# Feature attention and a gated MLP in one kernel: constants built on ScalarE or pinned later on VectorE, one load per step issued long ahead, crossbar transposes queued apart from their loads

## The chip, the cores and the metric

One core of one Trainium2 chip. The metric is the time of one execution on the device in microseconds (us); lower is better. Engines: PE is TensorE, DVE is VectorE, ACT is ScalarE, POOL is GpSimd, SP is SyncE. One digit of a slice in a profile is the share of busy time in tenths. The executions of the kernel before scatter widely: over the runs of this study, 296 to 307 us. So differences below 1% are told by spans of traces and by steps inside them, and a verdict on time only by ratios with an interval. A run is called slow when it lies over 1.5% above the fastest of the same kernel; ratios use the other, fast runs alone.

## The reference

```python
def phi(x):                                    # q, k: [8, 8, 576, 64]; w_phi: [64, 128]
    proj = np.einsum('bhsd,df->bhsf', x, w_phi)
    proj = proj - np.max(np.abs(proj), axis=-1, keepdims=True)
    return np.concatenate([np.exp(proj), np.exp(-proj)], axis=-1)
q_p, k_p = phi(q), phi(k)
kv = np.einsum('bhsf,bhsd->bhfd', k_p, v)
z = np.sum(k_p, axis=2)
num = np.einsum('bhsf,bhfd->bhsd', q_p, kv)
den = np.einsum('bhsf,bhf->bhs', q_p, z)[..., None] + 1e-06
x = (num / den).transpose(0, 2, 1, 3).reshape(8, 576, 512)
h = np.maximum(x @ w_in, 0.0)                  # w_in: [512, 1024]
u, v = h[..., :512], h[..., 512:]
v_n = (v - v.mean(-1)) / sqrt(var(v) + 1e-06)  # over the last axis
v_s = np.einsum('ts,bsd->btd', w_spatial, v_n) + b_spatial[None, :, None]
out = (u * v_s) @ w_out
```

## The kernel before

Of the 576 tokens of a batch, 512 form four *pair units* (two heads each); the last 64 tokens of two batches together form one *tail unit*. So there are 36 units, u0 to u35. One step of the program per unit: in step i, unit i's keys and queries are projected, later stages follow at fixed lags, and between them matmuls of the gated MLP (gMLP) of finished batches are dealt out as filler. The order within a step is `ORDER`, the dose of filler `RATE`. Tail units are u1, u9, u18 and u27; batch 4 begins at u19, batch 5 at u23, batch 6 at u28, batch 7 at u32.

Names in the profiles: k_bf, q_bf and v_f are the loaded keys, queries and values of a batch (k_tl, q_tl, v_tl of a tail unit); kT_b, qT_b (kT_t, qT_t of a tail) are their crossbar transposes, that is transposes made by a DMA. Up to batch 1 PE transposes them, and the result is copied to kT and qT. mk and mq are the maxima of keys and queries, kf and qf (qf_t) the exponentials, mhl the split of mq in two parts. em are the exponentials of mk, and vs (vst of a tail) is v scaled by them, x the normalised result of the attention and xT its transpose, w_spT the transposed w_spatial with the bias rows, ob a buffer for output rows. The feature lag is the number of steps between a unit's keys and its qf.

```python
    def load_heads(b, h0, n):                  # POOL loads and casts, SP transposes
        d = st[b]
        for x, t in (("k", k), ("q", q)):
            src = d[x][:, h0:h0 + n]
            pin(nc.gpsimd.dma_start)(out=src, in_=main_ap(t, b, h0, n))
            if b >= XB:
                pin(nc.sync.dma_start_transpose)(out=d[x + "T"][:, 2 * h0:2 * (h0 + n), :],
                                            in_=src.rearrange("p h x -> p (h x)"))
    # ... (cut)
    def a_split(u):
        m = mhl[u["i"] % NM]
        eng = nc.vector if u["i"] < EARLY else nc.gpsimd
        eng.tensor_copy(out=m[:, 0:H], in_=u["mq"])
        eng.tensor_tensor(out=m[:, H:2 * H], in0=u["mq"], in1=m[:, 0:H], op=ALU.subtract)
    # ... (cut)
    def o_mm(lhs, r):
        # ... (cut)
        ob = s2.tile([P, DM], FP32, tag="ob", name="ob", bufs=4)
        nc.scalar.copy(out=ob[r], in_=po[r])   # stored by SP; four buffers
        return ob
    # ... (cut)
    for i in range(NU + 4):
        u = unit(i)
        step(i)
        if i == 0:
            load(1)
            load_weights()
        if u and u["pair"] and u["pj"] == NP - 1 and u["b"] + 2 < B:
            load(u["b"] + 2)
        if u and u["pair"] and u["pj"] == TS and u["b"] % 2 == TB and u["g"] + 1 < G:
            load_tail(u["g"] + 1)
```

Of the kernel before, what the change touches and what calls it, by code (L numbers as in the profile page):

```python
# [16 lines left out]
def kernel(  # L17
# [40 lines left out]


    def pin(start):  # L60
        return lambda **kw: tc.keep_in_program_order(start(**kw))

    def main_ap(t, b, h0=0, n=H):
        return bass.AP(tensor=t.tensor, offset=t.offset + (b * H + h0) * S * D,
# [6 lines left out]
    st = {}  # L71
    gs = {}

    TS, TB = 1, 1
    XB = 2

    def load_tail(g):
        d = dict(
            q=ld.tile([P, H, D], BF16, tag="q_tl", name="q_tl", bufs=1),
            k=ld.tile([P, H, D], BF16, tag="k_tl", name="k_tl", bufs=1),  # L80
            v=ld.tile([P, H, D], FP32, tag="v_tl", name="v_tl", bufs=1),
        )
        gs[g] = d
        for x, t in (("k", k), ("q", q)):
            for i in range(2):
                pin(nc.gpsimd.dma_start)(out=d[x][i * TL:(i + 1) * TL], in_=tail_ap(t, 2 * g + i))
            if 2 * g >= XB:
                d[x + "T"] = ld.tile([P, NP, P], BF16, tag=x + "T_t", name=x + "T_t", bufs=1)
                pin(nc.sync.dma_start_transpose)(out=d[x + "T"], in_=d[x].rearrange("p h d -> p (h d)"))
        for i in range(2):  # L90
            pin(nc.sync.dma_start)(out=d["v"][i * TL:(i + 1) * TL], in_=tail_ap(v, 2 * g + i))

    def alloc(b):
        st[b] = dict(
            q=ld.tile([P, H, NB * D], BF16, tag="q_bf", name="q_bf", bufs=2),
            k=ld.tile([P, H, NB * D], BF16, tag="k_bf", name="k_bf", bufs=2),
            v=ld.tile([P, H * NB, D], FP32, tag="v_f", name="v_f"),
        )
        if b >= XB:
            for x in ("kT", "qT"):  # L100
                st[b][x] = ld.tile([P, 2 * H, P], BF16, tag=x + "_b", name=x + "_b", bufs=2)

    def load_heads(b, h0, n):
        d = st[b]
        for x, t in (("k", k), ("q", q)):
            src = d[x][:, h0:h0 + n]
            pin(nc.gpsimd.dma_start)(out=src, in_=main_ap(t, b, h0, n))
            if b >= XB:
                pin(nc.sync.dma_start_transpose)(out=d[x + "T"][:, 2 * h0:2 * (h0 + n), :],
                                            in_=src.rearrange("p h x -> p (h x)"))  # L110

    def load_v(b, eng):
        pin(eng.dma_start)(out=st[b]["v"].rearrange("p (h c) d -> p h (c d)", h=H), in_=main_ap(v, b))

    def load(b):
        alloc(b)
        load_heads(b, 0, H)
        load_v(b, nc.gpsimd if b < 2 else nc.sync)


    ident = cpool.tile([P, P], BF16)
    make_identity(nc, ident)
    alloc(0)
    for x, t in (("k", k), ("q", q)):
        first = s2.tile([P, 2, NB * D], FP32, tag="ob", name="first", bufs=4)
        nc.sync.dma_start(out=first, in_=main_ap(t, 0, 0, 2))
        nc.vector.tensor_copy(out=st[0][x][:, 0:2], in_=first)
    wphi2 = cpool.tile([P, 2 * F], BF16)
    nc.vector.memset(wphi2, 0.0)
    wphi_f = cpool.tile([P, F], FP32)  # L130
    for i in range(2):
        r = slice(i * D, (i + 1) * D)
        nc.sync.dma_start(out=wphi_f[r, :], in_=w_phi)
        nc.vector.tensor_copy(out=wphi2[r, i * F:(i + 1) * F], in_=wphi_f[r, :])
    load_tail(0)
    load_heads(0, 2, 2)
    load_v(0, nc.gpsimd)
    load_heads(0, 4, 4)

    w_in_bf = cpool.tile([P, KC, DFF], BF16)  # L140
    w_out_bf = cpool.tile([P, KC, DM], BF16)
# [5 lines left out]
    nc.sync.dma_start(out=bsp_row[TL:TL + 1, :], in_=moe_b_spatial)  # L147
    nc.sync.dma_start(out=bsp_row[0:1, :], in_=moe_b_spatial)

    def load_weights():  # L150
        pin(nc.gpsimd.dma_start)(out=w_in_bf, in_=moe_w_in.rearrange("(kc p) f -> p kc f", p=P))
        rows = moe_w_spatial[0:T0, :].rearrange("(p c) s -> p c s", c=NB)
        pin(nc.gpsimd.dma_start)(out=wsp, in_=rows[:, :, 0:T0])
        pin(nc.gpsimd.dma_start)(out=wspr, in_=rows[:, :, T0:S])
        pin(nc.gpsimd.dma_start)(out=wspt, in_=moe_w_spatial[T0:S, :])
        pin(nc.gpsimd.dma_start)(out=w_out_bf, in_=moe_w_out.rearrange("(kc p) f -> p kc f", p=P))


    sel1 = cpool.tile([P, H], BF16)
    sel = cpool.tile([P, H, F], BF16)  # L160
    nc.vector.tensor_tensor(out=sel1, in0=ident[:, 0:H], in1=ident[:, H:2 * H], op=ALU.add)
    nc.vector.tensor_scalar(out=sel, in0=sel1.unsqueeze(2).to_broadcast([P, H, F]), scalar1=-1.0,
                            scalar2=None, op0=ALU.mult)
    neghalf = cpool.tile([P, NB + 1], FP32)
    nc.vector.memset(neghalf, -0.5)


    NM = 3
    EARLY = 4
    XX = 9  # L170
    mhl, mT = [], []
    for i in range(NM):
        t = cpool.tile([P, P], BF16, name=f"mhl{i}")
        nc.vector.memset(t, 0.0)
        mhl.append(t)
        t = cpool.tile([P, P], BF16, name=f"mT{i}")
        nc.vector.memset(t, 0.0)
        mT.append(t)
    vst, vnt = [], []
    for i in range(2):  # L180
        t = cpool.tile([P, 2, 2, H, DA], BF16, name=f"vst{i}")
        nc.vector.memset(t, 0.0)
        vst.append(t)
        t = cpool.tile([P, 2, HALF], BF16, name=f"vnt{i}")
        nc.any.memset(t, 0.0)
        nc.any.memset(t[TL:TL + 1, 0, :], 1.0)
        nc.any.memset(t[0:1, 1, :], 1.0)
        vnt.append(t)
    nc.any.memset(w_spT[:, NB:NB + 2, :], 0.0)

    def transpose_spatial(i):

        pt = psum.tile([P, S], BF16, tag="bank", name="pt")
        if i < NB:
            sc = POS[i]
            for tp, c in enumerate(POS):
                nc.tensor.transpose(out=pt[:, tp * P:(tp + 1) * P], in_=wsp[:, c, bass.ds(sc, P, step=NB)],
                                    identity=ident)
            nc.tensor.transpose(out=pt[:, T0:S], in_=wspt[:, bass.ds(sc, P, step=NB)],
                                identity=ident[:TL, :TL])  # L200
            nc.vector.tensor_copy(out=w_spT[:, i, :], in_=pt)
            return
        for bl in range(2):
            lo = bl * TL
            for tp, c in enumerate(POS):
                nc.tensor.transpose(out=pt[lo:lo + TL, tp * P:(tp + 1) * P], in_=wspr[:, c, :], identity=ident)
            nc.tensor.transpose(out=pt[lo:lo + TL, T0:S], in_=wspt[:, T0:S], identity=ident[:TL, :TL])
            nc.vector.tensor_copy(out=w_spT[lo:lo + TL, NB + bl, :], in_=pt[lo:lo + TL, :])
        for bl, row in ((0, TL), (1, 0)):
            for pos, c in enumerate(POS):  # L210
                nc.vector.tensor_copy(out=w_spT[row:row + 1, NB + bl, pos * P:(pos + 1) * P],
                                      in_=bsp_row[row:row + 1, bass.ds(c, P, step=NB)])
            nc.vector.tensor_copy(out=w_spT[row:row + 1, NB + bl, T0:S], in_=bsp_row[row:row + 1, T0:S])


    def a_transpose(u):
        src = st[u["b"]] if u["pair"] else gs[u["g"]]
        if "kT" in src:
            for x in ("kT", "qT"):
                u[x] = src[x][:, 4 * u["pj"]:4 * u["pj"] + 4, :] if u["pair"] else src[x]  # L220
            return
        for x, copy in (("k", nc.scalar.copy), ("q", nc.vector.tensor_copy)):
            pt = psum.tile([P, 4, P], BF16, tag="bank", name="pt")
            for j in range(4):
                if u["pair"]:
                    blk = src[x][:, 2 * u["pj"] + j // 2, (j % 2) * P:(j % 2 + 1) * P]
                else:
                    blk = src[x][:, 2 * j:2 * j + 2, :]
                nc.tensor.transpose(out=pt[:, j, :], in_=blk, identity=ident)
            u[x + "T"] = a1.tile([P, 4, P], BF16, tag=x + "T", name=x + "T", bufs=2 if x == "k" else 4)  # L230
            copy(out=u[x + "T"], in_=pt)
# [296 lines left out]
    def unit(i):  # L528
        return units[i] if 0 <= i < NU else None
# [3 lines left out]
    def b_tasks(b):  # L533
# [15 lines left out]
        if tail:  # L549
# [5 lines left out]
            for x in bls:  # L555
                ts += [(mm, lambda j=j, x=x: b_o(2 * g + x, j)) for j in range(NB)]
        return ts

    ORDER = (("keys", 0.375), ("queries", 0), ("sums", 0), ("next", 0.125),
             ("attention", 0.5), ("features", 0), ("maxima", 0), ("out", 0))  # L560
    RATE = 3.23
    CAP = 1.76
    LAGS = dict(next=-1, maxima=1, features=2, sums=2, attention=3, out=4)
    FIRST = dict(next=-1, maxima=1, features=2, sums=2, attention=3, out=3)
    credit = [0.0]
# [1 line left out]
    def fill(share):  # L567
        credit[0] = min(credit[0] + RATE * share, CAP)
        while queue and credit[0] >= queue[0][0] / 2:
            cost, task = queue.pop(0)  # L570
            task()
            credit[0] -= cost

    def lag(u, what):
        return (FIRST if u["pair"] and u["b"] == 0 or u["i"] == 1 else LAGS).get(what, 0)

    def step(i):

# [32 lines left out]
    def finish_batch(u, f):  # L611
# [3 lines left out]
        elif bl == 1:  # L615
            f(g, [0, 1])

    for i in range(NU + 4):
        u = unit(i)
        step(i)  # L620
        if i == 0:
            load(1)
            load_weights()
        if u and u["pair"] and u["pj"] == NP - 1 and u["b"] + 2 < B:
            load(u["b"] + 2)
        if u and u["pair"] and u["pj"] == TS and u["b"] % 2 == TB and u["g"] + 1 < G:
            load_tail(u["g"] + 1)
    while queue:
        queue.pop(0)[1]()

# [29 lines left out]
```

## Time and profile before

| | before |
|---|---|
| median of the first 3 runs | 299.48 us (298.49 to 300.39) |
| span of the profiled run | 300.1 us |
| PE busy | 262.3 us |
| first gMLP product | 53.55 us |

The first gMLP product is the first matmul with w_in: from there PE has filler. The lines that bear the argument are in the prediction below. Here are two stretches that turn out to matter, from busy time by stretch (stretch and length; busy us and instructions of PE, weight loads, DVE, ACT, POOL; granted TensorE clock; DMA share; GB/s):

```profile
118.00:140.00 22.00, 18.33 (x207) 12.36 (x207) 12.80 (x34) 16.86 (x38) 12.58 (x23) 1.00 1.27 214
190.00:216.00 26.00, 24.17 (x278) 16.27 (x280) 18.49 (x45) 23.33 (x56) 14.30 (x27) 1.00 0.91 199
```

PE loses 3.7 and 1.8 us there, at full clock, though the DMA share is already 1.27 and 0.91.

### The profile page before, as it was taken

How to read it: one execution, taken by the hardware profiler on the slowest of the kernel's cores; microseconds unless marked ns; L12 is line 12 of the kernel's file. 1: busy time of each engine (PE TensorE's matmuls, PEld its weight loads, DVE VectorE, ACT ScalarE, POOL GpSimd, SP SyncE). 2: the span in 40 equal slices, each digit the busy share in tenths (PEclk: the TensorE clock that was granted, in tenths of full speed). 3: DMA queues.
4: the chain of work that ended last, by engine and by line, in shares of the span. 5: the costliest groups of instructions: out<-in, count | busy, mean ns of one | idle time of the engine just before them, and what ended most of it. 6: DMA issues, size and time to landing. Idle time of an engine off the chain costs nothing.

```text
span 300.1 us, 7883 instructions
## 1 busy us (share of the span) xinstructions
PE 262.3 (87%) x3007; PEld 180.4 (60%) x3046; DVE 211.9 (71%) x512; ACT 224.1 (75%) x512; POOL 184.1 (61%) x324
## 2 busy tenths in 40 slices
PE   2356888999999999779999995979999999999983
PEld 1235777576766766556667673656767667545441
DVE  5999889797968877549697883656788864445610
ACT  4336899878699997769999675879999837566033
POOL 9398388589635998447879962814988430048300
PEclk9999999999999999999999997999999999999998
DMA  9999999909952899999612999999303202600026
GB/s 142 245 153 268 166 111 159 262 1 123 215 190 75 109 166 233 152 280 162 136 21 28 185 211 224 142 305 235 81 1 37 20 2 69 226 26 0 0 84 233
DMA packets 82906, 41.10 MB, mean 137 GB/s; under 512 B 53490, under 2 KB 77234, under 8 KB 82868
## 3 DMA queue, kind: packets, MB, share of 16 engines
q1 hardware_dynamic: 55524, 27.08, 41.9%
q0 software_dynamic: 27344, 13.51, 33.1%
q8 instruction: 24, 0.39, 0.6%
q14 instruction: 14, 0.11, 0.1%
HBM read 32.85 MB, written 9.44 MB: 141 GB/s over the span
## 4 chain that ended last, share of the span: by engine, by line
PE 56%; DVE 16%; ACT 14%; DMA 8%; issue 3%; SPq 1%; ACTq 0%; DVEq 0%
PE ps L476 9%; PE pv L402 7%; PE pu L455 6%; PE po L499 6%; PE ps L236 6%; DMA out_dram<-ob 5%; ACT kf L251 5%; PE pn L353 3%; DVE mk L248 3%; DVE mq L257 3%; PE pv L333 3%; ACT qf L320 3%; PE pq L303 3%; PE pq L307 3%; PE ps L477 2%
## 5 line engine op out<-in xcount | busy, mean ns | idle before, releaser
L251 ACT ACTIVATE kf<-ps 128x512 bf16<-128x512 f32 x144 | 76.8, 667 | 19.4 <-DVE mk L248 19.1
L320 ACT ACTIVATE qf<-pq 128x512 bf16<-128x512 f32 x128 | 68.0, 667 | 13.6 <-PE pq L307 13.6
L268 POOL TENSOR_TENSOR vs<-v_f,em 128x512 bf16<-128x512 f32 x64 | 65.6, 1047 | 15.7 <-ACT em L263 15.5
L248 DVE TENSOR_REDUCE mk<-ps 128x4 f32<-128x512 f32 x72 | 46.1, 678 | 9.5 <-PE ps L236 9.2
L257 DVE TENSOR_REDUCE mq<-ps 128x4 f32<-128x512 f32 x72 | 46.3, 679 | 3.1 <-PE ps L236 2.7
L501 ACT COPY ob<-po 128x512 f32<-128x512 f32 (+1 forms) x37 | 21.6, 597 | 25.7 <-PE po L499 17.2
L405 DVE BATCH_NORM_STATS2 stats<-vr 128x6 f32<-128x512 bf16 (+1 forms) x37 | 25.2, 685 | 17.6 <-ACT vr L404 17.5
L402 PE MATMUL pv<-w_in_bf,xT 128*128 128x512 bf16 x119 | 31.2, 379 | 2.2 <-DMA xT<-x 1.7
L476 PE MATMUL ps<-w_spT,vn 128*128 128x512 bf16 x117 | 32.3, 379 | 0.6
L455 PE MATMUL pu<-xT,w_in_bf 128*128 128x512 bf16 x120 | 30.8, 379 | 0.7 <-DVE mq L257 0.3
L307 PE MATMUL pq<-mT,sel 128*128 128x128 bf16 x256 | 30.7, 222 | 0.0
L499 PE MATMUL po<-w_out_bf,uT 128*128 128x512 bf16 x121 | 29.7, 379 | 0.4 <-issue 0.2
L479 DVE TENSOR_TENSOR uT<-ps,uT 128x512 bf16<-128x512 f32 x32 | 22.1, 691 | 11.0 <-PE ps L477 9.7
L307 PEld LDWEIGHTS <-sel 128*128 128x128 bf16 x256 | 25.4, 99 | 6.5 <-issue 2.2
L344 DVE TENSOR_TENSOR x<-pn,rc 128x256 bf16<-128x256 f32 x64 | 25.8, 419 | 1.0
L287 POOL CAST mhl<-mq 128x8 bf16<-128x8 f32 x32 | 6.2, 192 | 33.1 <-DVE mq L257 29.3
L404 ACT ACTIVATE vr<-pv 128x512 bf16<-128x512 f32 (+1 forms) x37 | 23.2, 680 | 4.2 <-PE pv L402 3.3
L333 PE MATMUL pv<-vs,kf 128*128 128x66 bf16 x512 | 25.0, 195 | 0.0
L419 POOL TENSOR_SCALAR vn<-vr,rs 128x512 bf16<-128x512 bf16 x32 | 24.3, 772 | 0.8
L333 PEld LDWEIGHTS <-kf 128*128 128x128 bf16 x512 | 23.9, 99 | 1.0
L353 PE MATMUL pn<-kv,qf 128*128 128x66 bf16 x512 | 22.2, 193 | 2.0 <-ACT kf L251 0.9
L353 PEld LDWEIGHTS <-qf 128*128 128x128 bf16 x512 | 19.4, 97 | 6.0 <-issue 2.5
(127 smaller groups left out, 547.5 us busy)
## 6 DMA issues: line engine op xcount, KB each, us to landing
out_dram<-ob SPq DMA_DIRECT2D x32, 256.0 KB, 2.7
v_f<-in_v_dram SPq DMA_DIRECT2D x6, 1024.0 KB, 6.8
k_bf<-in_k_dram POOLq DMA_DIRECT2D x7, 512.0 KB, 6.7
q_bf<-in_q_dram POOLq DMA_DIRECT2D x7, 512.0 KB, 8.3
v_f<-in_v_dram POOLq DMA_DIRECT2D x2, 1024.0 KB, 8.5
v_tl<-in_v_dram SPq DMA_DIRECT2D x8, 128.0 KB, 4.2
w_in_bf<-in_moe_w_in_dram POOLq DMA_DIRECT2D x1, 1024.0 KB, 12.5
out_dram<-ob SPq DMA_DIRECT2D x8, 128.0 KB, 2.9
```

The source lines that it names most:

```text
L248: nc.vector.tensor_reduce(out=u["mk"][:, hs], in_=pk, axis=AX.X, op=ALU.max, apply_absolute_value=True)
L251: nc.scalar.activation(out=u["kf"][:, s, hs, :], in_=pk, func=AF.Exp, bias=0.0, scale=sc)
L257: nc.vector.tensor_reduce(out=u["mq"][:, 4 * half:4 * half + 4], in_=pq, axis=AX.X, op=ALU.max, apply_absolute_value=True)
L268: nc.gpsimd.tensor_tensor(out=vs[:, s, :, 0:D], in0=st[u["b"]]["v"][:, pj * H:(pj + 1) * H, :], in1=em[:, s, :].unsqueeze(2).to_broadcast( ...
L307: nc.tensor.matmul(out=pq[:, 2 * par + x, :], lhsT=sel[:, j, :], rhs=m, start=False, stop=(x == 1))
L320: nc.scalar.activation(out=qf[:, s], in_=pq, func=AF.Exp, bias=0.0, scale=sc)
L333: nc.tensor.matmul(out=pv[:, hh, s, :], lhsT=u["kf"][:, s, 4 * hh + c, :], rhs=u["vs"][:, s, 4 * hh + c, :], start=(c == 0), stop=False)
L353: nc.tensor.matmul(out=pn[:, pos, :], lhsT=u["qf"][hh][:, s, pos, :], rhs=d["kv"][:, 2 * u["pj"] + hh, s, :], start=(s == 0), stop=(s == 1))
L402: nc.tensor.matmul(out=pv[r], lhsT=lhs(kc), rhs=w_in_bf[:, kc, HALF:DFF], start=(kc == 0), stop=(kc == KC - 1))
L455: nc.tensor.matmul(out=pu, lhsT=w_in_bf[:, kc, dc * P:(dc + 1) * P], rhs=d["xT"][:, kc, :], start=(kc == 0), stop=(kc == KC - 1))
L476: nc.tensor.matmul(out=ps, lhsT=d["vn"][:, sp, cs], rhs=w_spT[:, sp, 0:T0], start=(sp == 0), stop=False)
L499: nc.tensor.matmul(out=po[r], lhsT=lhs(dc), rhs=w_out_bf[:, dc, :], start=(dc == 0), stop=(dc == KC - 1))
```

## The change

Its intent: (1) *constants*: get zero fills and casts out of VectorE's way at the start; (2) *loads and transposes*: spread the loads over the steps, long ahead, and queue the crossbar transposes so late that SP never sleeps behind its own loads; (3) *order*: new `ORDER`, `RATE`, `CAP`, and a feature lag of 3 for the first tail unit. The core of the diff (cuts marked; moved but equal lines left out):

```diff
-    def load_heads(b, h0, n):  ...            # load and crossbar transpose together
+    def cross(b):                             # crossbar transposes alone
+        d = st[b]
+        for x in ("k", "q"):
+            d[x + "T"] = ld.tile([P, 2 * H, P], BF16, tag=x + "T_b", name=x + "T_b", bufs=2)
+            pin(nc.sync.dma_start_transpose)(out=d[x + "T"], in_=d[x].rearrange("p h x -> p (h x)"))
 ...
-        nc.vector.memset(t, 0.0)              # vst
+        pin(nc.scalar.copy)(out=t.rearrange("p b s h d -> p (b s h d)"), in_=zero.to_broadcast([P, 4 * H * DA]))
 ...
-    EARLY = 4
+    EARLY = 6
+    EK = 7
+    AT, AB, XP, XQ = 6, 6, 3, 3
+    def constants(i):                         # on VectorE, after steps 1, 2 and 3
+        if i < 2:
+            for bl, row in ((0, TL), (1, 0)):
+                pin(nc.vector.tensor_copy)(out=vnt[i][:, bl, :], in_=ident[:, row:row + 1].to_broadcast([P, HALF]))
+        elif i == 2:
+            pin(nc.vector.memset)(w_spT[:, NB:NB + 2, :], 0.0)
 ...
-            for pos, c in enumerate(POS):     # bias casts: ten small ones become four
-                nc.vector.tensor_copy(out=w_spT[row:row + 1, NB + bl, pos * P:(pos + 1) * P], ...)
+            pin(nc.vector.tensor_copy)(
+                out=w_spT[r, NB + bl, 0:T0].rearrange("o (a b p) -> o a b p", a=2, b=2), ...)
 ...
-        for x, copy in (("k", nc.scalar.copy), ("q", nc.vector.tensor_copy)):
+        for x, copy in (("k", nc.vector.tensor_copy if u["i"] < EK else nc.scalar.copy), ("q", nc.vector.tensor_copy)):
 ...
-    ORDER = (("keys", 0.375), ("queries", 0), ("sums", 0), ("next", 0.125),
-             ("attention", 0.5), ("features", 0), ("maxima", 0), ("out", 0))
-    RATE = 3.23
-    CAP = 1.76
+    ORDER = (("keys", 0.375), ("queries", 0.25), ("sums", 0), ("attention", 0.25),
+             ("next", 0.125), ("features", 0), ("maxima", 0), ("out", 0))
+    RATE = 3.12
+    CAP = 2.11
 ...
+    for u in units:
+        if not u["pair"] and u["g"] > 0:
+            for n, (x, y) in enumerate((("k", 0), ("k", 1), ("q", 0), ("q", 1))):
+                at(u["i"] - AT + n, load_tail, x, u["g"], y)
+            ...
+            if 2 * u["g"] >= XB:
+                at(u["i"] - XQ, cross_tail, u["g"])
+        if u["pair"] and u["pj"] == 0 and u["b"] > 1:
+            at(u["i"] - AB, load, "k", u["b"])
+            at(u["i"] - AB + 1, load, "q", u["b"])
+            at(u["i"] - AB + 1, load_v, u["b"], nc.sync)
+            if u["b"] >= XB:
+                at(u["i"] - XP, cross, u["b"])
```

## The prediction

> **What bounds the kernel now.** I read the page's slices first, then busy time by stretch, then the chain of waits, then the waits of the stretches where TensorE (PE) is idle.
>
> ```profile
> PE   2356888999999999779999995979999999999983
> DVE  5999889797968877549697883656788864445610
> DMA  9999999909952899999612999999303202600026
> ```
>
> One digit is 7.5 us. PE is weak in the first six digits (45 us) and dips at 120 to 130, near 180 and near 195 us; elsewhere it is at 9. VectorE (DVE) is full where PE starts, and the DMA engines are busy there and in every dip. Busy time by stretch gives the sizes:
>
> ```profile
> 0.00:58.00 58.00, 37.87 (x460) 29.92 (x462) 49.80 (x121) 39.52 (x91) 41.75 (x69) 1.00 1.14 188
> 58.00:120.00 62.00, 61.18 (x756) 43.42 (x766) 50.62 (x124) 53.36 (x128) 46.76 (x84) 1.00 0.78 141
> 120.00:146.00 26.00, 21.74 (x283) 15.82 (x284) 17.47 (x46) 21.76 (x50) 16.38 (x29) 1.00 1.23 207
> 176.00:205.00 29.00, 23.58 (x300) 16.26 (x302) 16.23 (x40) 20.27 (x50) 14.06 (x24) 0.94 1.20 219
> ```
>
> PE idle is the length less the second number: 20.1 us before 58, 0.8 in the good stretch 58 to 120, 4.3 and 5.4 in the two bad ones. All of PE's idle time is 300.1 - 262.3 = 37.8 us; 5.9 more lies after 258 us, where only the last batch pair's products and stores remain. So the kernel is PE-bound, with a slow start and two stretches of stalls. What fills the start stands in the chain of waits, in order of time (start, us, what):
>
> ```profile
> 1.73 3.28 DMA wphi_f<-in_w_phi_dram
> ...
> 6.17 0.94 DVE vst L182
> 7.26 0.48 DVE vnt L186
> ...
> 9.24 0.69 DVE sel L162
> 9.93 0.33 DVE qT L231
> ...
> 15.14 0.96 DVE w_spT L213
> 16.12 1.05 DVE w_spT L211
> ...
> 53.55 1.37 PE pv L402 x5
> ```
>
> Up to 25 us the chain is DVE doing constants (vst, vnt, sel) and bias casts (w_spT) between the reduces that the pipeline needs. The copy of qT, ready to go at about 5.5 us, runs at 9.9. The last line is the first gMLP product; from there PE is rarely idle. The stalls later stand in the waits of PE, SyncE (SP) and ScalarE (ACT); the SP line is of the whole run, the others of 58 to 257 us (total, times, longest):
>
> ```profile
> PE ps L236 <- DMA kT_t<-k_tl: 5.1, 2, 3.4
> PE pv L402 <- DMA xT<-x: 1.7, 1, 1.7
> SPq L61 <- DMA k_bf<-in_k_dram: 75.8, 6, 39.5
> ACT ob L501 <- DMA out_dram<-ob: 5.4, 3, 2.8
> ```
>
> SP issues in order. A crossbar transpose (kT_b, kT_t) stands right behind its own load, so SP sleeps until the load has landed, and the xT transposes, v loads and output stores behind it sleep too.
>
> **What the Trainium skill says.** (1) "SBUF — State Buffer", Who interferes with whom: VectorE copies and casts in a 2-port mode and GpSimd (POOL) hold one port pair exclusively. The trace agrees: the 128x8 mhl cast takes 0.17 us at 13.45 and 1.27 us at 19.83, while POOL issues weight loads; the qT copy out of PSUM, at 19.50 in the same stretch, takes its usual 0.40. (2) "DMA: Bandwidth & Descriptors", Two DMAs through the same engine are not ordered: a DMA that reads what another wrote must have its issuing engine wait for the first one's semaphore. That is the 75.8 us above. (3) "ScalarE: Activation LUTs", Rules for kernel authors: about 0.3 us + 0.83 ns per element for one activation. The trace has 0.59 to 0.60 us for a 128x512 copy, less than the 0.72 of that rule. (4) "Perfetto Trace Analysis", Identifying the Most-Contended Engine: matmul busy time is no measure of distance from the peak. The trace agrees: 128x512 matmuls are recorded as 379 ns each, yet 16 of them take 3.45 us in the chain, 216 ns each. So I count PE's idle gains alone.
>
> **The change, part by part.**
>
> *Constants.* DVE loses two vst memsets (0.94 each), four vnt row memsets (0.48 each), two wphi casts (0.78 together) and ten bias casts (8 x 0.50 + 2 x 1.03 = 6.1), in all 10.7 us before 25 us. The bias casts become four, and move behind the spatial transposes, at about 50 us. ACT takes vst (two copies of 2112 elements: from 128x512 at 0.59 and 128x8 at about 0.20, some 0.77 ns per element, so an estimated 1.8 us each) and the wphi casts. DVE gains vnt as four 512-wide copies (estimate 0.4 each from the 0.42 of qT), spread over steps 1 and 2, and a memset of w_spT; also kT copies of seven units (0.33 each in the chain), and mhl (0.34) and kv (0.3) of two more units. So DVE's sum up to 45 us falls little, but what goes first changes. The order of instructions confirms it: sel is finished before the first load lands, and after the two casts of "first" come kT, qT and the reduces.
>
> *Hand run of the start,* by the new order on each engine, with durations of the trace. PE transposes at 4.2 as before; kT and qT copied by 5.8. ACT issues the wphi loads (1.2), loads its table (1.28), writes vst (1.8), so wphi2 is cast at 5.5 and second vst ends at 7.4: first kf at 7.5 (11.37 before). The tail unit's k and q are issued 0.8 us sooner, land at about 8.7; its kf at 11 (17.81 before). Third unit at 14.5 (25.16). Then POOL sets the pace: v_f lands at about 14.2 (15.0 before), vs of unit 0 takes 2.05, two issues 1.8, vst of the tail unit 4.5, three issues 2.7, vs 2.3, four issues 2.8, vs 2.3, ... so vs of units 2, 3, 4 are there at 27, 32 and 36 us (29.7, 34.2 and 41.1 before). PE, in order, waits for them, so kf of units 3, 4 fall to 21.5 and 28.3 (29.67, 35.35). From there ACT paces: kf 1.96 + qf 1.96 + em 0.2 + a little = 4.4 per unit, no longer the 4.9 (from 44.36 to 49.12) that kT and kv copies made of it. kf of unit 7 at 42.4 (49.12), first gMLP product at about 43.5 (53.5). That is 10 us. I take 8.5: the vnt copies and mhl casts will sometimes be caught by POOL's issues (about 1 us each time), and 7.75 MB must land by then.
>
> *Loads and transposes.* k and q are issued six and five steps ahead (a step is 6.0 to 6.3 us in the good stretch), in single issues, the crossbar transposes three steps ahead. SP should then find loads landed. The kT_t waits (5.1) should vanish, the xT wait (1.7) mostly, and of the ob waits the part that PE felt (0.95, and some of the 6.56 us store at 123 in the chain, together about 1.5). One flaw remains: q_tl's second half is issued in the very step that queues qT_t, so SP may still sleep some 5 us there. I take 6 of 8.3.
>
> *Filler rates.* RATE 3.23 to 3.12 moves 0.11 us x some 31 steps = 3.4 us of PE work from the pair stage to the end. PE is the bound in both: nothing. Nothing is added to ACT beyond 0.55 x 7 units less.
>
> Sum: 299.5 - 8.5 - 6 = 285.
>
> **The rivals.** (A) *POOL becomes the bound of the start.* It does vs, vst and every cast load in order[...]. For: in my hand run vs is gained by only 2 us for units 2 and 3, and POOL was busy 41.75 of 58 us. Against: 5 us are gained by unit 4, and POOL waited 29.3 us for mq of DVE. If it holds: start gains 4, total 289 to 290. (B) *The transfers only change places.* DMA busy share is over 1 in both bad stretches; earlier loads can collide with other stores, or w_in's second half and wsp come late at 45 to 50 us. For: the same bytes move. Against: from 60 to 70 us and in 205 to 258 the DMA queues are almost empty (share 0.04 and 0.29), so spreading has room. Then stalls give 1, total 290. (C) *ACT catches PE.* It is at 5.0 of 5 us in many stretches, but those follow stalls. My estimate of its need is 5.85 us per step against PE's 6.1; if it binds, 2 us are lost: 287. A and B together, 294.
>
> **Range and chances.** Hand run in full and all stalls gone: 299.5 - 10.5 - 8.3, some 280 to 281. One rival: 287 to 290. Both: 294. So 279 to 292. Faster by 2% is below 293.5; it needs 6 of 14.5 us: 0.89. Within 2%: 0.10. Slower: 0.01.
>
> **What would show it.** Right: first kf near 7.5, first mk reduce near 6.2; first gMLP product (pv from w_in) near 43.5 to 45; PE idle before 58 us down from 20 to about 12; SP's wait for k_bf under 20 us; no PE wait on kT_t above 1 us. DVE without w_spT casts before 40 us. Wrong: PE waiting for vs or vst from POOL for many us before 35 us (A); PE or ACT waits on out_dram, xT, qT_t or w_in of 3 us and more (B); more ACT-led chain after 60 us (C). A first gMLP product after 50 us would sink the prediction.

## The result, and the profile after

The kernel became slower: 309.10 us median of 4 runs (307.63 to 310.88) against 299.94 (298.49 to 305.65), ratio 1.0325, 95% interval 1.023 to 1.042. Ratios here are the mean time of one kernel's fast runs over that of the other's of the same rounds, so not quite the ratio of the medians. The span of the profiled run is 308.6 us.

The slices of the page after (one digit is 7.7 us now):

```profile
PE   3676788989999998199899999739999999999983
PEclk9955899999999999579999999968999999999999
DMA  9989999796875998993909998999301100610026
```

PE has two holes, at digits 17 and 27 (some 122 to 130 and 199 to 205 us), and after each hole the granted clock is down to half for a while. Busy time of the same two stretches as above:

```profile
118.00:140.00 22.00, 14.61 (x144) 9.57 (x143) 7.82 (x21) 11.05 (x25) 9.17 (x15) 0.77 1.12 188
190.00:216.00 26.00, 19.20 (x207) 12.34 (x204) 11.81 (x31) 17.03 (x41) 10.70 (x18) 0.87 1.24 207
```

144 matmuls are done in the stretch where there were 207, 207 where there were 278. To see where each microsecond goes I align the two traces by the start of the first exponential of keys of each unit (kf, on ACT):

| kf of | before, us | after, us | difference | 
|---|---|---|---|
| u0 | 11.37 | 7.58 | -3.79 |
| u2 | 25.16 | 14.61 | -10.55 |
| u4 | 35.35 | 33.36 | -1.99 |
| u8 | 56.57 | 54.92 | -1.65 |
| u10 | 71.15 | 72.16 | +1.01 |
| u18 | 124.03 | 122.49 | -1.54 |
| u19 | 132.68 | 139.02 | +6.34 |
| u26 | 174.90 | 181.96 | +7.06 |
| u28 | 191.57 | 193.94 | +2.37 |
| u29 | 200.85 | 208.49 | +7.64 |
| end | 300.07 | 308.60 | +8.53 |

Four things stand in it: a start gain of 10.55 us that is gone two units later; 2.7 us lost at u9 and u10; two stalls, of +7.9 us at u18 to u19 (a step of 16.53 us, 8.65 before) and +5.3 at u28 to u29 (14.55, 9.28 before); and gains just ahead of both (2.6 us from u10 to u18, 4.7 from u26 to u28), where the wait for kT_t of the kernel before is indeed gone.

The chain of waits after (start, us, what) shows the lost start:

```profile
17.77 2.05 POOL vst L287 x2
...
22.34 0.47 DVE vnt L61
22.82 1.19 DVE mk L257 x2
24.01 1.20 DVE mq L266 x2
...
26.07 0.92 DVE mhl L297
26.98 0.68 DVE x L353 x2
27.66 0.05 issue
27.71 0.61 PE pt L376 x4
...
33.36 2.06 ACT kf L260 x4
...
42.81 2.27 ACT kf L260 x4
...
46.28 1.29 DVE mk L257 x2
...
51.90 2.02 PE pv L411 x8
```

POOL's vst opens it, then VectorE works almost without a pause: a constant, the reduces, the split of the maxima (mhl, 0.92 us for 8 columns), the normalised x. PE, in order, transposes that x (L376) before it projects u4; from 27.71 to 32.84 us the chain is PE's, at half clock (a projection of 256 columns takes 421 ns there, 272 later). From 32.87 to 45.74 us it is ACT's alone: u4 to u7 are 13.94 us apart. Only from 46.28 to the first gMLP product at 51.90 is it VectorE's again. Later in the chain stand the bias casts, where the chain before had matmuls, and the two stalls:

```profile
65.79 1.89 DVE w_spT L61 x2
67.68 0.01 issue
67.69 1.57 DVE w_spT L61 x2
...
121.95 7.68 DMA qT_t<-q_tl
...
194.31 10.38 DMA out_dram<-ob
```

And the waits (total, times, longest), the first two lines of PE, the last of SP's own queue:

```profile
PE ps L245 <- DMA qT_t<-q_tl: 7.4, 1, 7.4
PE pt L301 <- ACT ob L510: 6.8, 1, 6.8
...
SPq L61 <- DMA k_bf<-in_k_dram: 12.3, 2, 10.0
```

The first stall: PE waits 7.4 us for the crossbar transpose of the tail's queries. SP issued it at 121.95, right behind the two transposes of batch 4, the second of which had waited for its load; and POOL had issued the 0.5 MB load of k of batch 5 at 120.81. The second: a store of 256 KB takes 10.4 us, so ACT has no free output buffer, and PE waits for ACT; k, q and v of batch 7 (0.5, 0.5 and 1 MB as they land) had been issued at 187.13, 190.49 and 192.08. SP's k_bf wait did fall, from 75.8 to 12.3 us.

The granted clock was 0.50 for 10.2 us from 124.9 and for 6.8 us from 203.4, 17.1 us in all after 33 us; before, it was so for 3.4 us (the last 2 us of the run, after the last matmul, left out). "TensorE: Matmul & The Clock Gate" of the Trainium skill (Part 1, What's actually happening) says that an idle window of some 3.4 us halves PE's clock until a busy window has passed; these traces agree, with stretches of 3.41 us before and of 6.83 and 10.24 us after. Half clock costs half of its length at most: (17.1 - 3.4) / 2 = 6.8 us, an estimate of what the stalls cost on top of the waiting. At the start the clock after is recorded as half from 15.7 to 32.8 us; the record of before begins only at 32.2, but its projections take the same 421 ns at 28 us.

### The profile page after: what moved, and what is told of

Read it like the earlier page. It is cut to its first block, busy times and chain, and to the rows that moved or that the text cites. A ratio compares the mean times of both kernels' runs of the same rounds, so it can differ in the third digit from the quotient of the medians.

```text
span 308.6 us, 7918 instructions
## 1 busy us (share of the span) xinstructions
PE 270.3 (88%) x3046; PEld 183.2 (59%) x3046; DVE 212.1 (69%) x517; ACT 223.2 (72%) x505; POOL 185.1 (60%) x322
## 4 chain that ended last, share of the span: by engine, by line
PE 68%; DMA 10%; ACT 8%; DVE 7%; POOL 3%; issue 1%; SPq 0%; ACTq 0%; POOLq 0%; DVEq 0%
PE pv L411 11%; PE pu L464 9%; PE ps L485 8%; PE ps L245 8%; PE po L508 8%; DMA out_dram<-ob 5%; PE pv L342 5%; PE pn L362 4%; PE pq L316 3%; PE pq L312 3%; ACT kf L260 3%; ACT qf L329 3%; DMA v_f<-in_v_dram 3%; DMA qT_t<-q_tl 2%; PE ps L486 2%
## 5 line engine op out<-in xcount | busy, mean ns | idle before, releaser
L414 DVE BATCH_NORM_STATS2 stats<-vr 128x6 f32<-128x512 bf16 (+1 forms) x37 | 24.5, 680 | 13.1 <-ACT vr L413 13.0
L508 PE MATMUL po<-w_out_bf,uT 128*128 128x512 bf16 x128 | 33.3, 405 | 0.0
L485 PE MATMUL ps<-w_spT,vn 128*128 128x512 bf16 x128 | 32.8, 379 | 0.0
L464 PE MATMUL pu<-xT,w_in_bf 128*128 128x512 bf16 x128 | 31.6, 379 | 0.0
L488 DVE TENSOR_TENSOR uT<-ps,uT 128x512 bf16<-128x512 f32 x32 | 22.0, 689 | 10.1 <-PE ps L486 8.4
L342 PE MATMUL pv<-vs,kf 128*128 128x66 bf16 x512 | 26.0, 198 | 1.5 <-POOL vs L277 1.5
L466 ACT ACTIVATE uT<-pu 128x512 bf16<-128x512 f32 x32 | 20.2, 666 | 5.5 <-PE pu L464 5.5
## 6 DMA issues: line engine op xcount, KB each, us to landing
q_bf<-in_q_dram POOLq DMA_DIRECT2D x6, 512.0 KB, 10.5
```

Of the source, the lines that this page charges most:

```text
L342: nc.tensor.matmul(out=pv[:, hh, s, :], lhsT=u["kf"][:, s, 4 * hh + c, :], rhs=u["vs"][:, s, 4 * hh + c, :], start=(c == 0), stop=False)
L464: nc.tensor.matmul(out=pu, lhsT=w_in_bf[:, kc, dc * P:(dc + 1) * P], rhs=d["xT"][:, kc, :], start=(kc == 0), stop=(kc == KC - 1))
L485: nc.tensor.matmul(out=ps, lhsT=d["vn"][:, sp, cs], rhs=w_spT[:, sp, 0:T0], start=(sp == 0), stop=False)
L508: nc.tensor.matmul(out=po[r], lhsT=lhs(dc), rhs=w_out_bf[:, dc, :], start=(dc == 0), stop=(dc == KC - 1))
```

## The experiments

Theories. **Start**: (P) POOL or ACT paces it, as the prediction had it; (D) VectorE paces it, from some 25 us to the first gMLP product. **Stalls**: (O) only the order of SP's queue is wrong; (Q) the store queues behind v's load on SP's own queue; (B) whatever stands beside the 0.5 and 1 MB loads, transpose or store, shares the 16 DMA engines with them and becomes slow. The expectations of the first four runs (e1_old_order, e2_old_loads, e6_tail_earlier, e4_v_later) have letters A and B of their own, told in each.

Eighteen runs, in five batches; in each the kernel before ran on the same chip, with medians of 301.8, 302.3, 302.2, 301.4 and 302.9 us. Two versions, e16_no_kq7 and e20_no_kq5, use wrong data on purpose. They still pass the comparison; I take it that the exponents are so small with these inputs that the features are nearly flat.

### Undoing parts

**e1_old_order**: the changed kernel with the third part undone.

```diff
-    ORDER = (("keys", 0.375), ("queries", 0.25), ("sums", 0), ("attention", 0.25), ("next", 0.125), ...
+    ORDER = (("keys", 0.375), ("queries", 0), ("sums", 0), ("next", 0.125), ("attention", 0.5), ...
-    RATE = 3.12; CAP = 2.11                   # and the feature lag FT of the first tail unit
+    RATE = 3.23; CAP = 1.76
```

> The changed kernel with the step order, RATE, CAP and the lag of the first tail unit of the kernel before; constants and loads as changed. Theory A (SyncE's in-order queue and the clustering of transfers make the loss): the two long stalls stay, time 304 to 310. Theory B (the new step order makes the loss: x transposes and qf_t ahead of the keys' features): kf of the fifth unit starts near 28 us instead of 33.4 and the time falls to 300 or below.

302.23 us (20 runs), ratio 0.993 (0.984 to 1.002), which rests on the two of its 20 runs that are fast. u4 comes at 29.49 instead of 33.36, so the third part (order, rates and lag together) costs 3.9 us there. But u6 is only 1.3 us ahead of the changed kernel: one subtract of 8 columns on VectorE takes 2.44 us beside POOL's vs. The first stall is short here (step 7.85 us instead of 16.53), with the same order on SP: there, qT_t was issued 1.5 us *before* the load of k of batch 5, in the changed kernel 1.1 us after it. The second stall is nearly whole (12.39). Its profiled run is one of its slow ones, so I use its steps, not its end.

**e2_old_loads**: the second part undone.

```diff
-    at(u["i"] - AB, load, "k", u["b"]) ...    # all of the at() block
+    at(u["i"], old_load, u["b"] + 2, nc.sync) # k, kT, q, qT, v together, as before
```

> The changed kernel with the load issues and crossbar transposes placed as in the kernel before (all weights, k, q and v of a batch at once, each transpose right behind its load). Theory A: the stalls of PE on qT_t (7.4 us) and of ScalarE on the output store (8 us) go, those of the kernel before (5.1 us on kT_t) come back; time 296 to 301. Theory B: time stays at 305 to 309.

305.31 us (20 runs), ratio 1.011 (1.008 to 1.014). The waits for kT_t are back (4.7 us) and one for xT of 8.3 us in the chain; step u18 to u19 is 11.21, u28 to u29 is 8.18, but u26 to u27 is 10.50. So both placements have stalls, in other places.

**e5_const_only**: both undone, the constants alone remain.

> The changed kernel with both other parts undone: loads and crossbar transposes placed as before, and the old order, rates and feature lag. Only the constants part is left. If that part alone gives what the prediction claimed for the start (8.5 us), the span is some 291 us; if the start gain is eaten at units 3 to 6 whatever the loads do (POOL's vs and vst, VectorE copies held by POOL), the time is that of the kernel before within 1%, kf of unit 8 at about 54 to 55 us, and the kT_t waits of 5 us are back.

303.86 us (4 runs), ratio 1.017 (1.004 to 1.030); the span is 300.6 us, as before. u3 is 8.5 us ahead of the kernel before, u4 4.9, u8 2.4, u11 1.7 behind. The start gain is eaten whatever the loads and the order do; the time, expected within 1% of the kernel before, is not shown to be better than it.

### What paces the start

**e8_order_mhl5**: tail loads one step earlier (e6_tail_earlier, below), the old order, and the split of unit 5's maxima on POOL.

```diff
-        eng = nc.vector if u["i"] < EARLY else nc.gpsimd
+        eng = nc.vector if u["i"] < 5 else nc.gpsimd
```

> On the version with tail loads one step earlier: the old order, rates and feature lag, and the split of the query maxima of unit 5 on POOL instead of VectorE (one cast and one subtract of 8 columns). Theory: with the old order alone unit 4 started at 29.5 us instead of 33.4, and that gain was lost at unit 6, where one 8-column subtract on VectorE took 2.44 us beside POOL's vs. If the held subtract was the cause, kf of unit 6 comes at 38 to 39 us (41.5 there, 42.7 in the version this is built on), and the gain of 2 to 3 us is still there at unit 10. Rival: another engine sets the pace there (ACT or POOL's vs); then unit 6 still comes after 40.5.

300.15 us (20 runs), ratio 1.000 (0.995 to 1.005). u6 at 41.28: the held subtract was *not* what kept it there. The chain of this run shows what did:

```profile
35.46 1.20 DVE mk L257 x2
36.66 1.20 DVE mq L266 x2
37.86 0.34 DVE kv L347
38.19 0.33 DVE kT L240
38.53 0.33 DVE qT L240
38.86 0.16 DVE rc L352 x2
39.02 0.73 DVE x L353 x2
...
40.23 0.24 DVE xT L377
...
51.03 1.05 PE pv L411 x4
```

That is one unit: 4.5 us of VectorE, nearly gapless (only a PE transpose of 0.41 us stands between), against the 4.4 us of ACT that the prediction had taken as the pace. It goes on until the first gMLP product at 51.03. In the changed kernel itself, with the later u4, ACT led over most of this stretch. Theory D, for this version; the next two runs test it.

**e14_short_mq**: 1 us of VectorE less per unit, u2 to u7; the maximum that is shortened cancels in the quotient.

```diff
-                                    in_=pq, axis=AX.X, op=ALU.max,
+                                    in_=pq[:, :, 0:8] if 2 <= u["i"] < 8 else pq, axis=AX.X, op=ALU.max,
```

> On the version with tail loads one step earlier, the old order and unit 5's split on POOL: in units 2 to 7 the maxima of the queries are taken over 8 features instead of 128 (the scale of a query's features cancels in the quotient, so the result stays right). This takes some 1.0 us per unit off VectorE, 6 us in all, and changes nothing else. Theory D (VectorE, not ACT or POOL, is the bound from 25 us to the first gMLP product; its reduces, copies and normalising stand in the chain there one after the other): the first gMLP product, 51.0 us there, comes 3 to 5 us earlier, at 46 to 48, until ACT's 4.4 us per unit binds. Rival (ACT or POOL paces the start, as the prediction had it): it moves by less than 1 us.

The first gMLP product comes 4.1 us earlier, in the chain of waits:

```profile
46.89 1.37 PE pv L412 x5
```

So D holds, and P falls for this stretch of this version; with VectorE relieved, POOL's vs (to 33 us) and then ACT and PE stand in the chain. 294.43 us (4 runs), ratio 0.986 (0.965 to 1.007), so unclear; u18 is 4.1 us ahead of e8_order_mhl5, u19 2.2, u28 2.4, u35 1.5: both stalls (steps 7.70 and 12.27, 5.72 and 11.36 there) took part of it.

**e15_kT_act**: the change itself had moved kT copies of seven units to VectorE. They go back to ACT.

```diff
-    EK = 7
+    EK = 0
```

> On the same version: the copies of kT of units 0 to 6 back on ACT, where they were before the change. Theory D (VectorE bound): VectorE loses 0.33 us per unit from unit 2 on, ACT gains 0.55; the first gMLP product comes 0.5 to 2 us earlier than 51.0 if ACT keeps up, and at worst at the same time. Rival (ACT paces): it comes 1 to 3 us later than 51.0.

298.48 us (20 runs), ratio 0.996 (0.990 to 1.001). The same line now:

```profile
47.89 1.37 PE pv L411 x5
```

3.1 us earlier than 51.03, more than expected: this piece of the change loaded the very engine that was the bound. u0 is 2.0 us late, as ACT is still filling vst; that did not matter. Of the 3.1 us little lasts: u11 and u18 are 1.6 us ahead of e8_order_mhl5, and u35 is 0.9 behind it, so in the whole time the gain is not shown.

### What makes the stalls

**e6_tail_earlier**: one number. In the built order, qT_t then stands ahead of batch 4's transposes.

```diff
-    AT, AB, XP, XQ = 6, 6, 3, 3
+    AT, AB, XP, XQ = 7, 6, 3, 3
```

> The changed kernel with AT 7 in place of 6: tail loads one step earlier, so that the built order has qT_t ahead of kT_b and qT_b on SyncE. Theory A: PE's wait for qT_t falls from 7.4 us to under 1, the step from unit 18 to 19 from 16.5 to about 7 us, the clock stays full there, and the time falls by 6 to 9 us, to about 301; the second stall (units 28 to 29) stays. If the wait only moves to another transfer, the time falls by less than 2 us.

298.79 us (20 runs), ratio 1.000 (0.994 to 1.005); span 296.0. Step u18 to u19 falls from 16.53 to 7.59 (8.65 before the change), and the clock is not halved again from 32.4 us until the last store. So the first stall, 7.9 us against the kernel before, is gone. The second stays (10.86), with a store of 8.51 us in the chain.

**e3_xp2**: the other way to the same order; no load moves.

```diff
-    AT, AB, XP, XQ = 6, 6, 3, 3
+    AT, AB, XP, XQ = 6, 6, 2, 3
```

> The changed kernel with the crossbar transposes of a batch queued one step later; no load moves. In the order of SyncE qT of the tail unit then stands ahead of kT and qT of the batch behind it. Theory O (the first stall is the order of SyncE's queue: qT of the tail stood behind two transposes of a batch, whose q had not landed): the step from unit 18 to 19 falls from 16.5 us to 9 or less, though the second stall stays, and the time by 5 to 8 us against the changed kernel's. Rival (the transfers are too many there whatever their order): the step stays over 12.

308.71 us (4 runs, two of them fast; the profiled one slow), ratio 1.026 (0.995 to 1.056). PE no longer waits for qT_t, which SP issued at 116.14, but step u18 to u19 is still 14.75: now a store takes 6.2 us, and the transposes of batch 4 come late. Theory O fails as a full account: the order named the victim, not the cause.

**e20_no_kq5**: the changed kernel, without the loads of k and q of batch 5; SP's order unchanged.

```diff
+        if b == 5:
+            return                            # st[5]["k"], st[5]["q"] are batch 4's
```

> The changed kernel, with k and q of batch 5 not loaded; batch 4's are used in their place (wrong data for batch 5, on purpose). The order of SyncE's queue stays, and qT of the tail stays behind q of batch 4. Theory B (shared DMA engines): qT of the tail, which took 7.7 us in the chain beside k of batch 5, takes 3 to 5, and the stores behind it are not slowed; the step from unit 18 to 19 falls from 16.5 to 11 to 13 us. Theory O (order alone: it is late because it stands behind q of batch 4): it is issued at the same time, takes as long, and the step stays at 15 or more.

qT_t is issued at about the same time (122.39 us, 121.95 there), and takes:

```profile
122.39 4.47 DMA qT_t<-q_tl
```

4.47 us instead of 7.68; step u18 to u19 is 9.90 instead of 16.53, better than expected, and the first two stores behind it land in 2.4 and 2.6 us (4.9 and 4.3 there). B at the first stall. 303.51 us (4 runs), ratio 1.017 (1.004 to 1.030): the second stall is whole there (14.06).

**e4_v_later**: the changed kernel with v two steps later.

```diff
-            at(u["i"] - AB + 1, load_v, u["b"], nc.sync)
+            at(u["i"] - AB + 3, load_v, u["b"], nc.sync)
```

> The changed kernel with each v load two steps later on SyncE, away from k and q of the same batch; the built order then also has qT_t ahead of kT_b for the third tail. Theory A: the store that took 10.4 us near 194 us lands in under 5, step 28 to 29 falls from 14.6 to 9 or less, the qT_t stall goes too, time 295 to 300. If the stall at 194 us has nothing to do with v: step 28 to 29 stays near 14, time about 301.

315.71 us (4 runs), ratio 1.048 (1.041 to 1.055). A clear miss: steps 15.77 and 16.18. v of batch 7 did leave the stores (issued at 213.34), but the order and times on SP changed with it, and now transposes stood beside k and q: PE waits 8.2 us for an xT issued at 124.75 (k and q of batch 5: 119.32 and 123.22), and in the chain qT_b takes 15.5 us from 191.40 (k and q of batch 7: 190.00 and 193.37). What is moved on a queue also moves what stands behind it.

**e9_v_pool**: e6 with v on POOL's queue.

```diff
-            at(u["i"] - AB + 1, load_v, u["b"], nc.sync)
+            at(u["i"] - AB + 1, load_v, u["b"], nc.gpsimd)
```

> On the version with tail loads one step earlier: v of batches 2 to 7 issued by POOL instead of SyncE, in the same step. Theory Q: the store of 8.5 us that ends the second stall waits behind v's 1 MB, issued on the same queue just before it; on another queue it takes 4 us or less, the step from unit 28 to 29 falls from 10.9 to about 7, and the time by 3 to 4 us. Rival theory B: stores are slow because all 16 DMA engines are shared with k, q and v whatever the queue; then the store stays at 7 us or more and the step stays over 9.5.

301.32 us (20 runs), ratio 1.005 (1.002 to 1.009). The first slow store starts at 185.85 and takes 6.93 us, *before* POOL issues v at 188.88; another takes 7.99 after it. Q falls. This is what "DMA: Bandwidth & Descriptors" of the Trainium skill says in Issuing engines are not separate DMA queues: all run on the same 16 engines and interleave, whoever starts them.

**e10_late_kq_early**: e6 with k and q of batches 5 and 7 two steps earlier.

```diff
-            at(u["i"] - AB, load, "k", u["b"])
+            at(u["i"] - AB - 2 * (u["b"] in (5, 7)), load, "k", u["b"])
 ...                                          # q, a step later, in the same way
```

> On the version with tail loads one step earlier: k and q of batches 5 and 7 loaded two steps earlier, so that they land before the stores of the pair before begin. Theory B (shared engines): the store at the second stall shortens from 8.5 to about 5 to 6 us, as only v's 1 MB is beside it, and the step from unit 28 to 29 from 10.9 to about 8. Theory Q (v ahead on the same queue): the store stays at 7.5 us or more and the step over 9.5.

The store takes 5.67 us, as B said. But the loads now stand beside the transposes of batch 6:

```profile
177.12 16.07 DMA kT_b<-k_bf
```

Steps u18 to u19 and u28 to u29 are 12.86 and 12.51, where 8 was expected of the second: the stall is back, on another transfer. 308.33 us (4 runs), ratio 1.032 (1.025 to 1.040), 9.5 us over e6_tail_earlier. It is the clearest picture of B: the load of q beside that transpose took 14.3 us as well.

**e16_no_kq7**: e6 without k and q of batch 7 (batch 6's are used).

> On the version with tail loads one step earlier: k and q of batch 7 are not loaded, batch 6's are used in their place (wrong result for batch 7, on purpose). v of batch 7 is still loaded. Theory B (the store at the second stall is slow because it shares the DMA engines with k and q): the store of 8.5 us falls to 4 to 6 us and the step from unit 28 to 29 from 10.9 to about 7 to 8; the time falls by some 3 us. Rival (v's load just ahead on the same queue, or the crossbar transposes of xT): the store stays over 7.5 us.

294.37 us (4 runs), ratio 0.987 (0.970 to 1.003), span 291.8. Step u28 to u29 is 7.92, and no store stands in the chain, though v is still loaded just ahead of them. Taking 1 MB of 2 away is enough.

**after_again**: the changed kernel once more.

> The changed kernel itself once more, beside the others on the same chip: some 307 to 311 us, 2 to 3.5% over the kernel before, with the step from unit 18 to 19 at 15 to 17 us and from unit 28 to 29 at 13 to 15 us, if both stalls belong to the kernel and not to one run's chance.

306.92 us (302.72 to 311.55, 4 runs), ratio 1.019 (0.989 to 1.049). Both stalls repeat: steps 14.81 and 13.65, qT_t 7.0 us and the store 8.75 in the chain. Only two of these runs are fast, so by themselves they leave the loss unclear; the first comparison (2.3 to 4.2%) shows it.

### A version that is faster

**e18_kq_far**: e6 with k and q of batch 7 at u21, where that trace's DMA engines were nearly idle.

```diff
-            at(u["i"] - AB, load, "k", u["b"])
-            at(u["i"] - AB + 1, load, "q", u["b"])
+            at(u["i"] - AB - 5 * (u["b"] == 7), load, "k", u["b"])
+            at(u["i"] - AB + 1 - 6 * (u["b"] == 7), load, "q", u["b"])
```

> On the version with tail loads one step earlier: k and q of batch 7 issued at unit 21, where the DMA engines moved 10 GB/s in that version's trace, instead of at units 26 and 27, ahead of the stores. Same bytes, right result. Theory B: as with no load of k and q at all, the step from unit 28 to 29 falls from 10.9 to about 8 us and the time by 3 us, if q of batch 6, issued 8 to 12 us behind, is not delayed into its transposes. If it is, the loss moves to units 25 to 28.

298.65 us (20 runs), ratio 0.993 (0.990 to 0.997). The store falls from 8.51 to 5.87, the step only from 10.86 to 10.57, and u22 and u23 lose 2.6 us. A miss: the loads of batch 6 behind them landed later (k in 11.3 us instead of 6.2, q in 10.1 instead of 6.0), so that batch's transposes slid 5 us, to the stores.

**e19_all**: that, with the old order, unit 5's split on POOL, and kT of u2 to u6 on ACT.

> That version, and the start with what the runs gave: the old order and rates, the split of unit 5 on POOL, kT copies of units 2 to 6 on ACT (units 0 and 1 on VectorE, as ACT is still building constants). The first gMLP product at 47.5 to 48.5 us, u10 about 4 us ahead of the kernel before, the second stall down to a step of 8 us; a time of 291 to 294 us, 2 to 3% below the kernel before. Rival: a stall returns elsewhere, as in each run that moved loads, and it is 296 or more.

295.85 us (4 runs), ratio 0.982 (0.949 to 1.014): u9 is 6.8 us ahead of the kernel before, u28 9.9, u29 7.3. The second stall is still there (11.87), with a store of 6.29 us behind v.

**e21_all_v_late**: that, with v of batch 7 behind the stores.

```diff
-            at(u["i"] - AB + 1, load_v, u["b"], nc.sync)
+            at(u["i"] - AB + 1 + 3 * (u["b"] == 7), load_v, u["b"], nc.sync)
```

> The joined version (e19_all), with v of batch 7 issued three steps later, after the stores of the pair before; it is first needed by POOL at unit 32 and by PE at unit 34. Theory B: no 0.5 or 1 MB load is then beside the stores; the store that took 6.3 us in the chain takes 3 to 5, the step from unit 28 to 29 falls from 11.9 to 8 to 10 us, and the time by 2 to 3 us, to some 293 (2.5 to 3% below the kernel before). Rival: the transposes of batch 6 beside the stores are enough to keep them slow, or v now comes late for units 32 to 34: no gain.

**293.46 us** (290.95 to 295.77, 6 runs) against 302.90, ratio **0.969 (0.963 to 0.976)**: faster than both kernels, with the right result. Step u28 to u29 is 8.18, the stores land in 2.3 to 2.8 us, and no half clock is granted between 24 and 290 us. SP's queue in the changed kernel (first fence) and here (second), at the stores of that place (start, us, SP's queue, what):

```profile
192.08 0.57 SPq L61 DMA_DIRECT2D v_f<-in_v_dram  x1
192.75 2.15 SPq L522 DMA_DIRECT2D out_dram<-ob  x2
194.99 1.02 SPq L516 DMA_DIRECT2D out_dram<-ob  x2
196.10 3.44 SPq L371 DMA_TRANSPOSE xT<-x  x1
199.63 6.11 SPq L516 DMA_DIRECT2D out_dram<-ob  x2
```

```profile
183.45 1.18 SPq L522 DMA_DIRECT2D out_dram<-ob  x2
184.72 1.04 SPq L516 DMA_DIRECT2D out_dram<-ob  x2
185.85 1.26 SPq L371 DMA_TRANSPOSE xT<-x  x1
187.20 1.01 SPq L516 DMA_DIRECT2D out_dram<-ob  x2
```

The third pair of stores spans 6.11 us in the changed kernel, as its second store waits for ACT to get a buffer; here 1.01.

**e22_v_late_only**: the same with k and q of batch 7 back ahead of the stores.

> The same with k and q of batch 7 back at units 26 and 27, just ahead of the stores. Theory B: without v but with k and q beside them the stores stay slow (7 us and more; in e9_v_pool the first slow store had k and q beside it and no v), the step from unit 28 to 29 is over 10.5 us, and the time is 1 to 3 us over e21_all_v_late's, less the 2.7 us that e18_kq_far lost at units 22 and 23.

294.13 us (6 runs), ratio 0.970 (0.965 to 0.976). The store is slow with k and q beside it, as expected (7.61 us), but the step is 9.09, under the 10.5 that I expected, and the time is the same. So either half of the loads taken away ends most of the stall, as in e16_no_kq7; a slow store alone isn't a stall: with four output buffers ACT waited for stores only 1.6 us here (8.0 in the changed kernel).

## Why the prediction was wrong

**The hand run up to u2 was right.** First kf 7.58 (7.5 predicted), u1 10.62 (11), u2 14.61 (14.5); first mk reduce 6.38 (near 6.2); SP's k_bf wait 12.3 us (under 20); no wait of PE on kT_t above 1 us; no w_spT casts before 40 us.

**"Then POOL sets the pace ... so kf of units 3, 4 fall to 21.5 and 28.3" is the step that failed in the start.** They came at 23.44 and 33.36. That is 5.0 of the 8.4 us by which the first gMLP product (51.90 us, not 43.5) missed; after 50 us it sinks the prediction by its own sign. After POOL's vst the chain shows VectorE, and then PE in order, at half clock. With the old order u4 starts at 29.49 (e1_old_order), so 3.9 of the 5.0 us are the third part of the change, of which the prediction took up the filler rate alone.

**The last step of the hand run was too short, by 3.5 us**: it left 1.1 us from kf of u7 to the first gMLP product, where the trace of before has 4.4 (49.12 to 53.55) and the one after 4.6. VectorE's reduces and normalising stand there.

**"From there ACT paces: ... 4.4 per unit", between the two, came out in the changed kernel**: 13.94 us from u4 to u7, 14.1 predicted, with ACT in the chain. It held only because u4 was late. With the old order VectorE is the bound, 4.5 us per unit in the chain of e8_order_mhl5: u4 came 3.6 us sooner there, the first gMLP product only 0.9, and 1 us less per unit on VectorE brought that forward by 4.1 us (e14_short_mq). The prediction added up ACT's and POOL's work per unit, never VectorE's, though it noted that "DVE's sum up to 45 us falls little". And what the change put on VectorE was not free: kT copies alone cost 3.1 us there (e15_kT_act). Of 8.5 us of start gain 1.65 were left at u8; PE's idle time before 58 us fell from 20.1 to 15.5 us, not to 12.

Two sums in it are off: 44.36 to 49.12 is 4.8 us and not 4.9, and 28.3 plus three times 4.4 is 41.5, not 42.4.

**The bias casts had a new place in the prediction ("at about 50 us") but no cost there.** They are in the chain at 65.79 with 3.48 us, beside POOL's vst, where PE could have been full; u8 to u10 lost 2.7 us. The port rule that the prediction cites first may be the reason, casts of VectorE held by POOL (argued, not tested): four casts of one partition take 3.48 us here, 4.42 in e21_all_v_late. No run moved the casts alone, so what they cost in time is read from the chain, not shown by a run. In five runs (e1_old_order, e2_old_loads, e5_const_only, e15_kT_act, e20_no_kq5) the clock is then halved for 3.4 us, from 68 to 72 us on: up to 1.7 us more, an estimate.

**"Stalls: I take 6 of 8.3" had the removal right and no term for what came instead.** The kT_t waits vanished: 2.6 us gained before u18 and 4.7 before u28. But step u18 to u19 grew by 7.9 and u28 to u29 by 5.3. Rival B, "the transfers only change places", was right, and the prediction had even named the spot (q_tl's second half and qT_t, "some 5 us"). But even as a rival it left the stalls a gain of 1 us, and nothing in the list made the kernel slower (a chance of 0.01). Its evidence against B was room at 60 to 70 and 205 to 258 us. The first was used (DMA share 0.84 and 1.14 in its two halves, 0.01 and 0.07 before), the second lies behind the last loads: 230 to 258 us stayed at 0.09. Neither is where the stalls were: there loads, transposes and stores meet, and the DMA share was already over 1. Moving loads forward by a step or two moved them onto transposes and stores; e20_no_kq5 (7.68 to 4.47 us), e10_late_kq_early (16.07 us) and e16_no_kq7 show it from three sides.

**Half clock was not in the sum at all.** 17.1 us of it after 33 us instead of 3.4, at most 6.8 us, by the working above.

**Rivals A and C**: POOL's vst opens the lost start (POOL 1.0 and 1.5 us of PE's waits), so A holds a small part. The 29.3 us of POOL's waiting that the prediction held against A are of the whole run; before 58 us they are 4.5. C, ACT as the bound after 60 us, was not seen.

What stays open: how much the bias casts cost by themselves; what the half clock of the start costs; whether VectorE's kT copies cost anything in the changed kernel itself, as e15_kT_act was built on the old order; and why e14_short_mq and e15_kT_act, with PE 3 to 4 us ahead, meet a second stall that is 0.9 and 1.5 us longer. I did not trace its transfers one by one.

## What to carry to other kernels

Add up the work per unit of *every* engine before naming the one that sets the pace, and ask of each moved instruction whether it lands on that engine. A load issued earlier is not free: look at what transposes and stores share the DMA engines in the steps where it will now run, and move it to a stretch that is empty, in small moves with a trace after each. A stall of PE like the two of some 7 us here can cost more than its length, as the clock was halved after both.

## What the Trainium skill lacked or had wrong

- "DMA: Bandwidth & Descriptors", Latency and other measured facts, gives 261 GB/s for a crossbar transpose. Here kT_b, 0.5 MB, lands in a median of 5.7 us in the changed kernel, 0.52 MB / 5.7 us = 92 GB/s (from issue to landing, with other transfers about, so not the rate of the transpose alone), and in 16.07 us in the chain beside two 0.5 MB loads. No page says how much a transpose slows beside loads.
- The same page's Rules for kernel authors advise to issue a DMA early and to wait late. They lack that the early place may be beside a store or transpose on the critical path: a 256 KB store took 10.38 us in the chain beside 2 MB of loads, where the median is 2.8.
- "SBUF — State Buffer", Who interferes with whom: agrees in kind; no page gives the size for tiny instructions. Two of 8 columns, some 0.17 us by themselves, took up to 2.44 us (e1_old_order), more than POOL's pair of instructions beside them (2.05).
- "TensorE: Matmul & The Clock Gate", Part 1: agrees (half clock in multiples of 3.41 us). What no page has: ahead of the first record of the clock the profile shows full clock. Before 32.2 us the kernel before shows 1.00, while its 256-wide projections take 421 ns at 28 us and 272 ns at 43 us.
